# A third buffer for a mixture's float32 weight loads, and gathers and scatters queued behind the last subtraction on GpSimd

## The chip, the cores and the metric

The kernel runs on one core of a Trainium2 chip. The metric is the device time of one execution in microseconds (us). The runs of the kernel before took 1203.83, 1204.78 and 1204.12 us, median 1204.12.

Names of the engines in the profile: PE is TensorE's matmuls and PEld its weight loads, DVE is VectorE, ACT is ScalarE, POOL is GpSimd, SP is SyncE, which here only issues DMAs.

## What is computed

The reference, cut to what matters. The input x has shape (4, 2496, 256), which is 9984 tokens of 256.

```python
x = np.fft.fft(np.fft.fft(x, axis=1), axis=2).real            # over the sequence, then over the 256

# first mixture: 8 experts, each takes 1248 tokens
order = np.argsort(-(x @ w_gate).flatten())                   # greedy, best (token, expert) pairs first
...                                                           # a token once, an expert 1248 times
for e in range(8):
    out[mask[e]] = np.maximum(x[mask[e]] @ w1[e], 0) @ w2[e]  # 256 -> 1024 -> 256

# second mixture, on the first's output
e_idx = np.argmax(x @ w_gate2, axis=1)
for e in range(8):
    out[e_idx == e] = gate_w * sigmoid(x @ w_output_gate)[:, e] * (np.maximum(x @ w1[e], 0) @ w2[e])
```

## The kernel before

Up to about 250 us the kernel computes the transform and the scores of the first mixture's gate. Then a selection finds, expert by expert, which 1248 tokens an expert takes; it runs on VectorE with some matmuls (L525 to L542, the places of the tokens at L669 to L671). From 760 to 1164 us the second mixture runs. Between the two lies the stretch that the change touches: the first mixture's eight experts, one after the other, and beside them the preparation of the second.

Matrices are kept as two float16 halves, a high one and a low one (the rest), and each product takes three matmuls. So each tile that is copied costs a pass for the high half and one for the low half.

For each expert k of the first mixture (class Moe1):

- `prepare` loads its six float32 weight tiles (wf, `Weights.part`, L756, issued by SP; which expert is a number that the chip works out, so an ISA instruction reads it first), waits in the plan for the selection, and gathers the tokens by index in ten indirect DMAs that POOL issues (xg, L873). The tokens go to the layers in three chunks of 384, 384 and 480. Transposes (L890) and their copies by ACT and DVE (L892, L893) make xt of each chunk.
- `weights` cuts the wf tiles into halves (wh; a part of it on POOL, L788).
- `hidden` runs the first layer in eight units per chunk (matmuls L824 into ph, three PSUM buffers). ACT makes the high half (ht, L904). The low half is made by DVE (L910), or, in the odd units for which `fk // 2 < HP[k]`, by POOL: ACT copies once more into hf (L907, three buffers) and POOL subtracts (L908). HP is 3, 3, 3, 4, 2, 0, 0, 0 for experts 0 to 7.
- `out_block` runs the second layer (matmuls L832 into py, two PSUM buffers), and ACT copies each result to yr (L921).
- `route` picks the second mixture's expert for each token, writes the results to DRAM (yd, SP, L970 and L971), works out each token's place in the second mixture's lists (L979), and puts entries of eight bytes there in ten indirect DMAs that POOL issues (lst, L985).

Beside it `keep2` (L1083 to L1109) prepares the second mixture's weights: 8 experts of 4 parts, 32 parts of 512 KB in float32. SP loads a part into one of two buffers (`g_0`, `g_1`, L756), ACT makes its high half (wp, L1102), DVE the low half (L1103), and SP stores both halves to DRAM (wsd, L1104). The load of part n + 2 is issued behind the store of part n, so that it finds the buffer free.

```python
nc.scalar.activation(h[:, q, 0], fs[q], AF.Copy, scale=64.0)
nc.vector.scalar_tensor_tensor(h[:, q, 1], fs[q], 64.0, h[:, q, 0], op0=OP.mult, op1=OP.subtract)
nc.sync.dma_start(self.wsd[e, :, q], h[:, q])
if e < 7 or q < 2:
    load(e + q // 2, (q + 2) % 4)
```

What sets the order of the work: the program is traced with a planner's clock. The matmul units of the first mixture advance the clock (`flow.unit`), and the side jobs above are generators that yield how long they want to wait on it. So the numbers yielded (GY, SY, KY and the like) set between which units a step is queued; nothing on the chip waits for them. A scheduler then orders each engine's instructions. `issue_after(i)` in it places an instruction behind i in the queue; that too is an order, not a wait. The loads of `keep2` are placed behind the latest of the first mixture's weight loads (`self.W.at`).

Of the kernel before, what the change touches and what calls it, by code (L numbers as in the profile page):

```python
# [10 lines left out]
F32 = mybir.dt.float32  # L11
# [715 lines left out]
GG = 8.0  # L727
RY = 5.0
GY = 2.0
SY = 2.5  # L730
XY = 2.0
KY = 7.0
# [103 lines left out]
class Moe1:  # L836
    CH = ((0, 3), (3, 3), (6, 4))

    def __init__(self, tc, nc, a, xd, yd, lst, wsd, sel, pools, consts, bufs):
        self.tc, self.nc, self.a, self.xd, self.yd, self.lst, self.sel = tc, nc, a, xd, yd, lst, sel  # L840
        self.P = pools
        self.c = consts
        p = pools["keep"]
        self.base = p.tile([128, 8], F32, name="m_base")
        nc.vector.tensor_copy(self.base, consts["eoff"])
        self.wg = p.tile([128, 2, 2, 16], F16, name="m_wg")
        self.scat = []
        self.W = Weights(nc, pools["wts"], pools["stage"], a["moe_w1"], a["moe_w2"], a["moe_w2t"])
        self.wsd, self.bufs = wsd, bufs
        self.W2 = Weights(nc, pools["wts"], pools["stage"], a["moe2_w1"], a["moe2_w2"])  # L850
# [10 lines left out]
    def load(self, k):  # L861
        e = self.nc.sync.value_load(self.sel.ei[0:1, k:k + 1], min_val=0, max_val=7)
        return self.W.load(e)

    def gather(self, k):
        nc = self.nc
        idx = self.sel.idx[k]
        xg = self.P["xg"].tile([128, 10, D], F32, name="xg")

        def steps():  # L870
            for t in range(10):
                m = 128 if t < 9 else 96
                nc.gpsimd.indirect_dma_start(out=xg[:m, t], out_offset=None, in_=self.xd,  # L873
                                             in_offset=bass.IndirectOffsetOnAxis(ap=idx[:m, t:t + 1], axis=0))
                yield
        return xg, steps()

# [20 lines left out]
    def hidden(self, xt, n, wh, k):  # L898
        nc = self.nc
        ht = self.P["ht"].tile([128, 2, 8, 512], F16, name="ht")  # L900
        for fk in range(8):
            ph = self.P["psum"].tile([128, 512], F32, name="ph", bufs=3)
            ffn1_unit(nc, xt, wh[0], fk, n, ph[:, :n])
            self.act = nc.scalar.activation(ht[:, 0, fk, :n], ph[:, :n], AF.Relu)  # L904
            if fk % 2 and fk // 2 < HP[k]:
                hf = self.P["work"].tile([128, 480], F32, name="hf", bufs=HFB)
                nc.scalar.activation(hf[:, :n], ph[:, :n], AF.Relu)  # L907
                nc.gpsimd.tensor_sub(ht[:, 1, fk, :n], hf[:, :n], ht[:, 0, fk, :n])  # L908
            else:
                nc.vector.scalar_tensor_tensor(ht[:, 1, fk, :n], ph[:, :n], 0.0, ht[:, 0, fk, :n],  # L910
                                               op0=OP.max, op1=OP.subtract)
            yield n * 6 / 2400.0
        self.ht = ht
# [10 lines left out]
    def route(self, yr, k):  # L924
# [54 lines left out]
        nc.vector.tensor_copy(pi, px)  # L979
        nc.vector.tensor_add(self.base, self.base, pr[:, 80:88])  # L980
        self.counted = k
        ent = self.lst.rearrange("r (s w) -> (r s) w", w=2)
        for t in range(10):
            m = 128 if t < 9 else 96
            s = nc.gpsimd.indirect_dma_start(out=ent, in_=en[:m, t], in_offset=None,  # L985
                                             out_offset=bass.IndirectOffsetOnAxis(ap=pi[:m, t:t + 1], axis=0))
            for o in self.scat:
                self.tc.declare_no_dep(s.ins, o.ins, reason="every row has a place of its own")
            self.scat.append(s)
            yield 2.0 if k == 6 else 8.0 if k == 7 else 4.0  # L990

    def ffn(self, k, flow):

        wh = self.ws.pop(k)
        xg, xt = self.xgs.pop(k)
        yr = self.P["yr"].tile([128, 10, YW], F32, name="yr")
        self.nc.gpsimd.memset(yr[96:128, 9], 0.0)
        hts, nxt = {}, []

        def unit(d):  # L1000
            flow.unit(d)
            while nxt and nxt[0][0] <= 0:
                if next(nxt[0][1], 1):
                    nxt.pop(0)
                    self.cut += 1
                break
            if nxt:
                nxt[0][0] -= 1

        for c in range(4):  # L1010
            if c < 3:
                cur = xt
                if c < 2:
                    xt, st = self.xt(xg, c + 1)
                    nxt.append([3, st])
                for d in self.hidden(cur[0], cur[1], wh, k):
                    unit(d)
                hts[c] = self.ht
            else:
                self.tail = k  # L1020
            if c > 0:
                flow.until(lambda: self.gated >= k)
                t0, nt = self.CH[c - 1]
                for t in range(nt):
                    m = min(128, CAP - (t0 + t) * 128)
                    for d in self.out_block(hts[c - 1], t0 + t, t * 128, m, wh, yr):
                        unit(d)

        def rest():
            yield from self.route(yr, k)  # L1030
            self.routed = k
        flow.add(rest(), 1.0, prio=PR)
# [8 lines left out]
    def prepare(self):  # L1041

        for k in range(8):
# [4 lines left out]
                self.sel.placed = k  # L1048
            yield lambda: self.sel.placed >= k
            xg, steps = self.gather(k)  # L1050
            for t, _ in enumerate(steps):
                yield 0.0 if t < 4 else GY
            yield lambda: self.tail >= k - 1
            xt, steps = self.xt(xg, 0)
            for _ in steps:
# [1 line left out]
            self.xgs[k] = (xg, xt)  # L1057
            yield lambda: k in self.ws
            self.ready = k

    def weights(self):

# [19 lines left out]
    def keep2(self):  # L1082

        nc = self.nc
        yield lambda: self.at >= KEEP[0]
        h = self.P["wts"].tile([128, 4, 2, 1024], F16, name="wp", bufs=1)
        fs = [self.bufs[q % 2].rearrange("p a b -> p (a b)")[:, :1024] for q in range(4)]

        def load(e, q):
            with self.tc.issue_after(self.W.at.ins):  # L1090
                self.W2.part(fs[q], slice(e, e + 1), q)

        load(0, 0)
        load(0, 1)
        for e in range(8):
            if e and KEEP[e] > self.at:
                yield lambda: self.at >= KEEP[e]
            else:
                yield KY
            for q in range(4):  # L1100
                with self.tc.issue_after(self.act.ins):
                    nc.scalar.activation(h[:, q, 0], fs[q], AF.Copy, scale=64.0)  # L1102
                nc.vector.scalar_tensor_tensor(h[:, q, 1], fs[q], 64.0, h[:, q, 0], op0=OP.mult, op1=OP.subtract)  # L1103
                nc.sync.dma_start(self.wsd[e, :, q], h[:, q])  # L1104
                if e < 7 or q < 2:
                    load(e + q // 2, (q + 2) % 4)
                if q < 3:
                    yield KY
            self.kept = e  # L1109

    def run(self, flow, m2):
        self.cut = 0
        self.gated = -1
        self.counted = self.kept = -1
# [430 lines left out]
```

## Time and profile before

| | |
|---|---|
| median of the runs | 1204.12 us |
| the profiled execution | 1203.47 us, of which the span is 1201.7 us |
| PE busy | 1119.0 us (93%), 9823 matmuls |
| PEld busy | 821.8 us (68%) |
| DVE busy | 729.9 us (61%) |
| POOL busy | 498.4 us (41%) |
| ACT busy | 440.8 us (37%) |
| moved by DMA | 212.96 MB, mean 177 GB/s |

The span runs from the first to the last instruction that the profiler shows; 1.8 us of the execution lie around it. Busy times are those of each engine over the span; engines overlap. All times in the text count from the span's start. The granted clock is a share of TensorE's full clock, 1.00 being 2.4 GHz and 0.50 being 1.2 GHz.

### The profile page before, as it was taken

To read this page: it belongs to the slowest core of one execution; us is meant where nothing else is said; L and a number is where in the kernel's file an instruction comes from. 1 tells how busy PE (TensorE), PEld (TensorE's weight loads), DVE (VectorE), ACT (ScalarE), POOL (GpSimd) and SP (SyncE) were. 2 spreads that over 40 slices of the span, in tenths; PEclk is the share of its full clock that TensorE was granted. 3 is DMA by queue.
4 is the path that set the end of the run, shared out by engine and by line. 5 is a ranking of instruction groups with operands and counts; after the bars stand their busy time and mean duration, and the time that the engine had idled before them with its cause. 6 is when DMAs were issued, how large, how long until landed. Compare 5 with 4: busy or idle time off the path is not lost.

```text
span 1201.7 us, 24544 instructions
## 1 busy us (share of the span) xinstructions
PE 1119.0 (93%) x9823; PEld 821.8 (68%) x9823; DVE 729.9 (61%) x1786; ACT 440.8 (37%) x936; POOL 498.4 (41%) x471
## 2 busy tenths in 40 slices
PE   7998879979898989899798999999999999999998
PEld 4653546756667657567485767766766799999997
DVE  5866779897978977867456574434334343434343
ACT  3423334263452734345354443222223122222221
POOL 3825351468373781433306045643332334343331
PEclk8999989999999999989899999999999999999999
DMA  7834722243341571686838458444343366788782
GB/s 257 334 122 157 264 80 88 61 128 65 106 90 64 155 182 56 150 271 155 239 129 244 162 134 295 139 157 153 119 172 114 119 250 234 273 311 331 308 332 92
DMA packets 80036, 212.96 MB, mean 177 GB/s; under 512 B 11850, under 2 KB 48986, under 8 KB 69168
## 3 DMA queue, kind: packets, MB, share of 16 engines
q1 hardware_dynamic: 65360, 180.46, 44.5%
q0 software_dynamic: 14560, 30.91, 8.5%
q8 instruction: 78, 1.28, 0.5%
q14 instruction: 38, 0.31, 0.1%
HBM read 162.22 MB, written 50.42 MB: 177 GB/s over the span
## 4 chain that ended last, share of the span: by engine, by line
PE 28%; issue 23%; DVE 16%; POOL 10%; DMA 9%; ACT 2%; POOLq 0%; SPq 0%; DVEq 0%; ACTq 0%
PE py L832 14%; PE ph L824 9%; DMA g<-moe_w 6%; DMA out<-ot,tbrow 3%; POOL xg L1336 3%; POOL out L1381 2%; POOL g L1336 2%; DVE s_msk L525 2%; DVE ht L910 2%; PE px L693 1%; POOL xg L873 1%; DVE wp L1103 1%; PE pt L890 1%; POOL lst L985 1%; PE sp L531 1%
## 5 line engine op out<-in xcount | busy, mean ns | idle before, releaser
L832 PEld LDWEIGHTS <-ht 128*128 128x128 f16 (+1 forms) x3912 | 380.6, 99 | 61.3 <-issue 6.0
L824 PE MATMUL ph<-xt,wh 128*128 128x384 f16 (+4 forms) x2352 | 386.1, 316 | 26.9 <-DVE ht L910 14.8
L832 PE MATMUL py<-wh,ht 128*128 128x272 f16 (+2 forms) x3264 | 393.8, 277 | 4.2 <-ACT yr L921 4.2
L824 PEld LDWEIGHTS <-wh 128*128 128x128 f16 x2352 | 211.2, 99 | 148.8 <-issue 38.8
L1368 ACT ACTIVATE ht<-ph 128x512 f16<-128x512 f32 x166 | 99.1, 597 | 315.8 <-PE ph L824 315.8
L1369 DVE SCALAR_TENSOR_TENSOR ht<-ph,ht 128x512 f16<-128x512 f32 x166 | 114.8, 691 | 126.7 <-ACT ht L1368 126.7
L985 POOL DMA_INDIRECT lst<-r_en,r_pi x80 | 87.5, 1094 | 145.5 <-DVE r_pi L979 89.5
L904 ACT ACTIVATE ht<-ph 128x384 f16<-128x384 f32 (+1 forms) x192 | 98.4, 516 | 85.0 <-PE ph L824 76.9
L1381 POOL DMA_INDIRECT out<-ot,tarow x54 | 54.5, 1010 | 158.8 <-DVE ot L1380 152.1
L873 POOL DMA_INDIRECT xg<-xd,s_idx x80 | 87.9, 1099 | 34.9 <-issue 20.8
L910 DVE SCALAR_TENSOR_TENSOR ht<-ph,ht 128x384 f16<-128x384 f32 (+1 forms) x147 | 85.0, 585 | 19.4 <-ACT ht L904 19.1
L908 POOL TENSOR_TENSOR ht<-hf,ht 128x384 f16<-128x384 f32 (+1 forms) x45 | 48.7, 1090 | 93.2 <-ACT hf L907 80.0
L305 PE MATMUL big<-y,tab 128*128 128x36 f16 (+3 forms) x660 | 79.4, 273 | 1.1 <-DVE y L256 1.1
L921 ACT ACTIVATE yr<-py 128x272 f32<-128x272 f32 x80 | 31.3, 394 | 121.0 <-PE py L832 103.6
L832 PE MATMUL py<-wp,ht 128*128 128x256 f16 x648 | 73.7, 273 | 0.0
L824 PE MATMUL ph<-xt,wp 128*128 128x256 f16 (+2 forms) x624 | 72.9, 277 | 0.0
L1381 POOL DMA_INDIRECT out<-ot,tbrow x29 | 28.9, 997 | 101.9 <-DVE ot L1380 96.1
L1380 DVE TENSOR_SCALAR ot<-py,g 128x256 f32<-128x256 f32 x45 | 21.7, 483 | 70.6 <-PE py L832 70.6
L824 PEld LDWEIGHTS <-wp 128*128 128x128 f16 x624 | 51.4, 98 | 19.1
L1103 DVE SCALAR_TENSOR_TENSOR wp<-g,wp 128x1024 f16<-128x1024 f32 x32 | 39.9, 1247 | 32.2 <-ACT wp L1102 32.1
L305 PEld LDWEIGHTS <-tab 128*128 128x128 f16 x660 | 38.8, 97 | 30.0 <-issue 3.0
L525 DVE SCALAR_TENSOR_TENSOR s_msk<-s_vv,lo,s_jw 128x1280 f16<-128x1280 f32 x35 | 57.5, 1643 | 0.8
(254 smaller groups left out, 1313.2 us busy)
## 6 DMA issues: line engine op xcount, KB each, us to landing
wh<-wsd SPq DMA_DIRECT2D x50, 1024.0 KB, 6.0
wp<-wsd SPq DMA_DIRECT2D x26, 1024.0 KB, 6.0
wf<-moe_w SPq DMA_DIRECT2D x32, 512.0 KB, 6.0
g<-moe_w SPq DMA_DIRECT2D x32, 512.0 KB
wsd<-wp SPq DMA_DIRECT2D x32, 512.0 KB, 5.1
xa<-xa SPq DMA_DIRECT2D x8, 1280.0 KB, 11.1
xd<-xr SPq DMA_DIRECT2D x20, 512.0 KB, 4.8
yd<-yr SPq DMA_DIRECT2D x8, 1156.5 KB
```

What stands on the lines that cost most here:

```text
L305: self.nc.tensor.matmul(dst, self.tabs[par][k][:, cs, c, u], self.y[par][:, cs, w, c, bs, qs], start=(n == 0), stop=(n == 3 * NCH - 1))
L525: nc.vector.scalar_tensor_tensor(m, self.vv[:, :, None].to_broadcast(sh), lo, self.jw[:, r, None, :].to_broadcast(sh), op0=OP.subtract, op ...
L824: Flow.pe = nc.tensor.matmul(dst, w1[:, dk, a, fk * 128:fk * 128 + 128], xt[:, b, dk, :n], start=(k == 0), stop=(k == 5))
L832: Flow.pe = nc.tensor.matmul(dst, ht[:, a, fk, t0:t0 + m], w2[:, fk // 4, b, fk % 4], start=(fk == 0 and a == 0 and b == 0), stop=(fk == 7 ...
L873: nc.gpsimd.indirect_dma_start(out=xg[:m, t], out_offset=None, in_=self.xd, in_offset=bass.IndirectOffsetOnAxis(ap=idx[:m, t:t + 1], axis=0))
L904: self.act = nc.scalar.activation(ht[:, 0, fk, :n], ph[:, :n], AF.Relu)
L910: nc.vector.scalar_tensor_tensor(ht[:, 1, fk, :n], ph[:, :n], 0.0, ht[:, 0, fk, :n], op0=OP.max, op1=OP.subtract)
L985: s = nc.gpsimd.indirect_dma_start(out=ent, in_=en[:m, t], in_offset=None, out_offset=bass.IndirectOffsetOnAxis(ap=pi[:m, t:t + 1], axis=0))
L1336: nc.gpsimd.indirect_dma_start(out=g[:, h], out_offset=None, in_=self.yd, in_offset=bass.IndirectOffsetOnAxis(ap=row[:, 0, u + h:u + h + 1 ...
L1368: nc.scalar.activation(hi, src, AF.Relu)
L1369: nc.vector.scalar_tensor_tensor(lo, src, 0.0, hi, op0=OP.max, op1=OP.subtract)
L1381: st = nc.gpsimd.indirect_dma_start(out=self.out, in_=ot, in_offset=None, out_offset=bass.IndirectOffsetOnAxis(ap=row[:, 1, u + h:u + h + ...
```

## The change

There are three parts to it.

1. A third buffer for the float32 parts of the second mixture (tile `k_2`). Part n uses buffer n mod 3. The load of part n + 3 is issued after the conversion of part n, ahead of that part's store; before, part n + 2 was issued behind it. The load is still placed behind the latest weight load of the first mixture.
2. Each gather and each scatter is placed behind the last subtraction (L908) traced so far on POOL (`behind`).
3. The planner's steps for gathers and scatters. For experts 1 to 7 three gathers are placed first, and the other seven are a side job of their own, 3 us of the planner's clock apart (2 for expert 1). The transposes of the second and third chunk are traced only when all ten gathers are. The scatters of experts 0 to 5 begin 7 us later in the plan, and stand 3.5 rather than 4 apart.

```diff
@@ steps of the plan
+GL = 3.0
+SD = 7.0
@@ class Moe1
+    def behind(self):
+        return self.tc.issue_after(self.sub.ins) if self.sub else ExitStack()
@@ gather (each of ten)
-                nc.gpsimd.indirect_dma_start(out=xg[:m, t], out_offset=None, in_=self.xd,
+                with self.behind():
+                    nc.gpsimd.indirect_dma_start(out=xg[:m, t], out_offset=None, in_=self.xd,
@@ hidden
-                nc.gpsimd.tensor_sub(ht[:, 1, fk, :n], hf[:, :n], ht[:, 0, fk, :n])
+                self.sub = nc.gpsimd.tensor_sub(ht[:, 1, fk, :n], hf[:, :n], ht[:, 0, fk, :n])
@@ route (ten scatters)
+        if k < 6:
+            yield SD
-            s = nc.gpsimd.indirect_dma_start(out=ent, in_=en[:m, t], in_offset=None,
+            with self.behind():
+                s = nc.gpsimd.indirect_dma_start(out=ent, in_=en[:m, t], in_offset=None,
...
-            yield 2.0 if k == 6 else 8.0 if k == 7 else 4.0
+            yield 2.0 if k == 6 else 8.0 if k == 7 else 3.5
@@ ffn
                 if c < 2:
+                    flow.until(lambda: self.got[k] == 10)
                     xt, st = self.xt(xg, c + 1)
@@ prepare
-            for t, _ in enumerate(steps):
-                yield 0.0 if t < 4 else GY
+            self.got[k] = 0
+            if k:
+                for _ in range(3):
+                    next(steps)
+                    yield GY
+                self.flow.add(self.others(k, steps), GL)
+            else:
+                for t, _ in enumerate(steps):
+                    yield 0.0 if t < 4 else GY
+                self.got[k] = 10
...
+    def others(self, k, steps):
+        for t in range(3, 10):
+            next(steps)
+            self.got[k] = t + 1
+            yield GL if k > 1 else GY
@@ keep2
-        fs = [self.bufs[q % 2].rearrange("p a b -> p (a b)")[:, :1024] for q in range(4)]
+        fs = [t.rearrange("p a b -> p (a b)")[:, :1024] for t in self.bufs]
+        fs.append(self.P["keep"].tile([128, 1024], F32, name="k_2", bufs=1))
-        def load(e, q):
+        def load(n):
             with self.tc.issue_after(self.W.at.ins):
-                self.W2.part(fs[q], slice(e, e + 1), q)
+                self.W2.part(fs[n % 3], slice(n // 4, n // 4 + 1), n % 4)
-        load(0, 0)
-        load(0, 1)
+        for n in range(3):
+            load(n)
...
+                n = 4 * e + q
+                f = fs[n % 3]
...
+                if n < 29:
+                    load(n + 3)
                 nc.sync.dma_start(self.wsd[e, :, q], h[:, q])
-                if e < 7 or q < 2:
-                    load(e + q // 2, (q + 2) % 4)
```

How the order of the instructions moves is shown at three places. In the names a part's buffer is g_2072 (buffer 0), g_2073 (1) and k_5714 (the new one); a part's shape is 128x1024 or 128x4x256.

SP's queue at the turn from expert 3 to expert 4, before: the first mixture's last weight loads (wf), the store of the results (yd), and the loads of parts 13 (g_2073) and 14 (g_2072).

```order
L1104 DMA wsd<-wp 128x2048
L756 ISA
L756 DMA wf<-moe_w2t 128x1024
L970 DMA yd<-yr 128x9x257
L756 ISA
L756 DMA wf<-moe_w2t 128x1024
L756 DMA g_2073<-moe_w 128x1024
L756 DMA g_2072<-moe_w 128x4x256
L971 DMA yd<-yr 96x257
```

The same place now, with the loads of parts 14 (k_5714), 15 (g_2072) and 16 (g_2073).

```order
L1135 DMA wsd<-wp 128x2048
L758 ISA
L758 DMA wf<-moe_w2t 128x1024
L758 ISA
L758 DMA wf<-moe_w2t 128x1024
L758 DMA k_5714<-moe_w 128x4x256
L758 DMA g_2072<-moe_w 128x4x256
L977 DMA yd<-yr 128x9x257
L978 DMA yd<-yr 96x257
L758 DMA g_2073<-moe_w 128x1024
```

Part 13's load has gone ahead of the expert's last weight loads, parts 14 and 15 stand where 13 and 14 stood, and the store of the results stands behind them.

ACT's queue at the same turn, before: the conversions L1102 are of parts 13, 14, 15 and 16, and L921 copies results of the second layer (yr).

```order
L904 ACTIVATE ht<-ph 128x384 x2
L799 ACTIVATE wt<-wf 128x256
L1102 ACTIVATE wp<-g_2073 128x1024
L921 ACTIVATE yr<-py 128x272
L1102 ACTIVATE wp<-g_2072 128x1024
L921 ACTIVATE yr<-py 128x272 x2
L904 ACTIVATE ht<-ph 128x480
L1102 ACTIVATE wp<-g_2073 128x1024
L904 ACTIVATE ht<-ph 128x480 x4
L1102 ACTIVATE wp<-g_2072 128x1024
```

The same place now, where the conversions (L1131) are of parts 14, 15 and 16.

```order
L801 ACTIVATE wt<-wf 128x256
L911 ACTIVATE ht<-ph 128x384
L899 ACTIVATE xt<-pt 128x480
L911 ACTIVATE ht<-ph 128x384 x2
L1131 ACTIVATE wp<-k_5714 128x1024
L1131 ACTIVATE wp<-g_2072 128x1024
L928 ACTIVATE yr<-py 128x272 x3
L911 ACTIVATE ht<-ph 128x480 x5
L1131 ACTIVATE wp<-g_2073 128x1024
```

Part 13's conversion has moved some ten instructions ahead and stands above these rows; those of 14 and 15 stand together ahead of three copies of results, and 16 behind five units of the third chunk.

POOL's queue where it gathers the tokens of expert 4 (index tile s_idx_90) while expert 3 computes, before: gathers are L873, scatters L985, subtractions L908.

```order
L788 TENSOR_TENSOR wh<-wf,wh 128x2x256
L985 DMA lst<-r_en,r_pi 81920x2
L908 TENSOR_TENSOR ht<-hf,ht 128x384
L985 DMA lst<-r_en,r_pi 81920x2 x2
L873 DMA xg<-xd,s_idx_90 128x256 x8
L908 TENSOR_TENSOR ht<-hf,ht 128x384
L873 DMA xg<-xd,s_idx_90 128x256
L908 TENSOR_TENSOR ht<-hf,ht 128x384
L873 DMA xg<-xd,s_idx_90 96x256
L985 DMA lst<-r_en,r_pi 81920x2
L997 MEMSET yr 32x272
```

The same place now (gathers L880, scatters L995, subtractions L915).

```order
L880 DMA xg<-xd,s_idx_90 128x256 x3
L915 TENSOR_TENSOR ht<-hf,ht 128x384
L995 DMA lst<-r_en,r_pi 81920x2
L1007 MEMSET yr 32x272
L915 TENSOR_TENSOR ht<-hf,ht 128x384
L880 DMA xg<-xd,s_idx_90 128x256
L995 DMA lst<-r_en,r_pi 81920x2
L880 DMA xg<-xd,s_idx_90 128x256 x2
L995 DMA lst<-r_en,r_pi 81920x2
L880 DMA xg<-xd,s_idx_90 128x256
L995 DMA lst<-r_en,r_pi 81920x2
L915 TENSOR_TENSOR ht<-hf,ht 128x480
```

Eight gathers stood in a row ahead of a subtraction; three do now, and the others have moved behind the subtractions and alternate with the scatters.

## Rows read from the trace of the kernel before

**Rows 1.** Stage table, last stage and whole span: stretch, us, busy us, PEclk, DMA share, GB/s.

```profile
760.00:1164.10 404.10, 403.62 (x3514) 322.67 (x3512) 159.33 (x265) 105.82 (x187) 147.62 (x145) 1.00 0.58 216
...
sum 1201.70, PE 1118.98 PEld 821.79 DVE 729.94 ACT 440.80 POOL 498.42; mean PE 124.33 PEld 91.31 DVE 81.10 ACT 48.98 POOL 55.38
```

**Rows 2.** Waits of PE, 490 to 660: us in total, times, longest.

```profile
PE ph L824 <- DVE ht L910: 10.0, 3, 6.6
PE ph L824 <- ACT hf L907: 5.4, 1, 5.4
PE py L832 <- ACT yr L921: 4.2, 3, 2.5
```

**Rows 3.** Waits of ACT, whole span.

```profile
ACT wp L1102 <- DMA g<-moe_w: 40.2, 17, 8.3
...
ACT hf L907 <- POOL ht L908: 7.7, 2, 5.3
```

**Rows 4.** Timeline of PE: start, us, engine, line, operation, [idle before <- releaser].

```profile
373.82 0.19 PE L542 MATMUL sp<-r,ch 128*128 128x8 f16 x1 [3.07 <-DVE r L538]
...
440.70 0.56 PE L824 MATMUL ph<-xt,wh 128*128 128x480 f16 x2 [3.79 <-ACT hf L907]
...
457.10 0.49 PE L890 MATMUL pt<-cf,xg 128*128 128x128 f32 x3
...
512.82 2.56 PE L824 MATMUL ph<-xt,wh 128*128 128x480 f16 x6 [5.43 <-ACT hf L907]
...
570.30 2.94 PE L832 MATMUL py<-wh,ht 128*128 128x272 f16 x24 [1.57 <-ACT yr L921]
...
586.45 4.96 PE L824 MATMUL ph<-xt,wh 128*128 128x480 f16 x12 [6.58 <-DVE ht L910]
...
655.50 1.38 PE L824 MATMUL ph<-xt,wh 128*128 128x480 f16 x6 [1.82 <-DVE ht L910]
```

**Rows 5.** Timeline of ACT, conversions of parts 6, 7, 13 and 14.

```profile
506.54 1.06 ACT L1102 ACTIVATE wp<-g 128x1024 f16<-128x1024 f32 x1 [4.99 <-DMA g<-moe_w]
...
510.79 1.06 ACT L1102 ACTIVATE wp<-g 128x1024 f16<-128x1024 f32 x1 [2.45 <-DMA g<-moe_w]
...
568.90 1.06 ACT L1102 ACTIVATE wp<-g 128x1024 f16<-128x1024 f32 x1 [0.92 <-DMA g<-moe_w]
...
573.11 1.06 ACT L1102 ACTIVATE wp<-g 128x1024 f16<-128x1024 f32 x1 [2.86 <-DMA g<-moe_w]
```

**Rows 6.** Timeline of SP, loads of part 6, and of parts 13 and 14.

```profile
494.10 1.24 SPq L756 DMA_DIRECT2D g<-moe_w  x1
...
558.66 2.35 SPq L756 DMA_DIRECT2D g<-moe_w  x2
```

**Rows 7.** Windows of 4 us: stretch, us, busy us, PEclk, DMA share, GB/s.

```profile
440.00:444.00 4.00, 3.30 (x20) 1.59 (x20) 2.57 (x6) 3.92 (x9) 3.67 (x4) 0.72 0.17 58
...
512.00:516.00 4.00, 3.18 (x9) 1.32 (x9) 3.85 (x11) 1.81 (x5) 3.08 (x4) 0.50 0.89 263
516.00:520.00 4.00, 4.00 (x30) 1.97 (x28) 1.85 (x3) 2.90 (x7) 3.09 (x4) 0.89 1.02 400
...
560.00:564.00 4.00, 4.00 (x30) 2.81 (x29) 3.96 (x9) 2.51 (x5) 3.29 (x3) 1.00 1.15 216
...
584.00:588.00 4.00, 1.55 (x4) 0.56 (x4) 2.92 (x4) 1.95 (x4) 1.30 (x3) 0.50 0.89 323
588.00:592.00 4.00, 4.00 (x23) 1.76 (x22) 1.88 (x2) 2.07 (x5) 0.00 (x0) 0.50 0.44 151
```

**Rows 8.** Timeline of POOL, two of the gathers for expert 4.

```profile
438.16 0.95 POOL L873 DMA_INDIRECT xg<-xd,s_idx  x1 [0.30 <-issue]
...
442.27 1.85 POOL L873 DMA_INDIRECT xg<-xd,s_idx  x1 [0.16 <-ACT wp L1102]
```

**Rows 9.** Timeline of DVE, the shift at L670 twice.

```profile
369.36 1.02 DVE L670 TENSOR_SCALAR pi<-pi 128x80 int32<-128x80 int32 x1
...
514.38 0.20 DVE L670 TENSOR_SCALAR pi<-pi 128x80 int32<-128x80 int32 x1
```

More of the change, by code (lines that the diff above doesn't have):

```diff
@@ L846, in __init__ @@
         self.wg = p.tile([128, 2, 2, 16], F16, name="m_wg")
-        self.scat = []
+        self.scat, self.sub = [], None
         self.W = Weights(nc, pools["wts"], pools["stage"], a["moe_w1"], a["moe_w2"], a["moe_w2t"])
@@ L872, in steps @@
                 m = 128 if t < 9 else 96
-                nc.gpsimd.indirect_dma_start(out=xg[:m, t], out_offset=None, in_=self.xd,
-                                             in_offset=bass.IndirectOffsetOnAxis(ap=idx[:m, t:t + 1], axis=0))
+                with self.behind():
+                    nc.gpsimd.indirect_dma_start(out=xg[:m, t], out_offset=None, in_=self.xd,
+                                                 in_offset=bass.IndirectOffsetOnAxis(ap=idx[:m, t:t + 1], axis=0))
                 yield
@@ L984, in route @@
             m = 128 if t < 9 else 96
-            s = nc.gpsimd.indirect_dma_start(out=ent, in_=en[:m, t], in_offset=None,
-                                             out_offset=bass.IndirectOffsetOnAxis(ap=pi[:m, t:t + 1], axis=0))
+            with self.behind():
+                s = nc.gpsimd.indirect_dma_start(out=ent, in_=en[:m, t], in_offset=None,
+                                                 out_offset=bass.IndirectOffsetOnAxis(ap=pi[:m, t:t + 1], axis=0))
             for o in self.scat:
@@ L1100, in keep2 @@
             for q in range(4):
+                n = 4 * e + q
+                f = fs[n % 3]
                 with self.tc.issue_after(self.act.ins):
-                    nc.scalar.activation(h[:, q, 0], fs[q], AF.Copy, scale=64.0)
-                nc.vector.scalar_tensor_tensor(h[:, q, 1], fs[q], 64.0, h[:, q, 0], op0=OP.mult, op1=OP.subtract)
+                    nc.scalar.activation(h[:, q, 0], f, AF.Copy, scale=64.0)
+                nc.vector.scalar_tensor_tensor(h[:, q, 1], f, 64.0, h[:, q, 0], op0=OP.mult, op1=OP.subtract)
+                if n < 29:
+                    load(n + 3)
                 nc.sync.dma_start(self.wsd[e, :, q], h[:, q])
-                if e < 7 or q < 2:
-                    load(e + q // 2, (q + 2) % 4)
                 if q < 3:
@@ L1111, in run @@
     def run(self, flow, m2):
+        self.got, self.flow = {}, flow
         self.cut = 0
```

## The prediction

> **What bounds the kernel now.** I read the stage table first. TensorE (PE) is busy 1118.98 of 1201.70 us, so 82.7 us are all that better ordering can give back; the stage from 760 to 1164 has 0.5 us of them [rows 1]. So I read next who stops PE between 490 and 660, the stretch in which ScalarE (ACT) converts most of the second mixture's 32 float32 weight parts: 10.0, 5.4 and 4.2 us, 19.6 in all [rows 2]. All three releasers are ACT, or VectorE behind ACT: PE stands because ACT's queue stands. In the table of waits ACT stands for the parts' loads (g<-moe_w) for 40.2 us in 17 waits, the longest 8.3 [rows 3]. The second line there is another cause: ACT waits 7.7 us for a buffer that GpSimd's (POOL's) subtraction at L908 must free.
>
> The stalls themselves stand in PE's timeline: 3.07 us before 373.82, 3.79 before 440.70, 5.43 before 512.82, 6.58 before 586.45 and 1.82 before 655.50 [rows 4]. On ACT, part 6 is converted at 506.54 and part 7 at 510.79, each after a wait for its load; parts 13 and 14 at 568.90 and 573.11 likewise [rows 5]. SP issued part 6 at 494.10, and parts 13 and 14 together at 558.66 [rows 6]; before that they stood in SP's queue behind the first mixture's last weight load.
>
> A stall costs a second time. In 512 to 516 the granted clock is 0.50, which is 1.2 of 2.4 GHz, after PE had stood 5.4 us; a busy microsecond there does half the work. The loss, busy time times the missing share, is 3.18 x 0.5 + 4.00 x 0.11 = 2.0 us after the stall at 512; (1.55 + 4.00) x 0.5 = 2.8 us after the one at 586; 3.30 x 0.28 = 0.9 us after the one at 440 [rows 7].
>
> **The change, part by part.** *Third buffer.* No conversion, load or store is added; each load moves one conversion earlier on SP. A load can only start when the conversion three before it has freed its buffer, and SP stands for that with the store behind it; that store is next needed in the second mixture, so I cost this wait at nothing. What it buys depends on which load is late.
> - Stall at 512: part 6 is now issued before SP reaches the first mixture's last weight load, and part 7 takes part 6's place at 494.10. Part 6 landed 12.4 us after that [rows 5, 6]. If part 7 does the same, ACT leaves its conversion at 507.6 instead of 511.85, 4.3 us earlier, and 1.2 us of the stall stay; if the fewer scatters in that stretch help, none. I take 1.0: gain 5.4 - 1.0 = 4.4, and 2.0 of clock. Bounds: 3.2 without the clock, 7.4.
> - Stalls from 568 to 587: part 13 is loaded and converted ahead; parts 14 and 15 are issued ahead of the big result store and take, at worst, the places of 13 and 14, which landed at 568.90 and 573.11 [rows 5]. The order on ACT now has both conversions ahead of three result copies (yr) that PE waits for. So the 6.6 us go, and with them the smaller wait for L910 just before (10.0 - 6.6 - 1.8 = 1.6 [rows 2, 4]); the wait for yr, 4.2 - 2.5 - 0.2 = 1.5 [rows 2], may stay, or grow until part 15 is converted: PE stood from 570.30 - 1.57 = 568.73 on [rows 4], so 573.11 + 1.06 - 568.73 = 5.4. I take 2.0 left of 9.7, nearer to the present 1.5 than to 5.4, as the store of the results no longer stands in front. Gain 7.7, clock 2.8 less 0.5: 10.0. Bounds 9.7 - 5.4 = 4.3, and 9.7 + 2.8 = 12.5.
> - Stalls at 642 and 655: part 22 takes the place of 21 and waits as that did, so the 2.5 us for yr stay; part 23 is early and the 1.8 us go. Bounds 0 and 4.3.
> - Moved conversions: parts 13 and 21 now stand between the first layer's units, where a conversion costs ACT 1.06 us [rows 5] with PE and VectorE both full. I take 1.0 for both; bounds 0 and 2 x 1.06.
>
> How fast a load lands decides half of this. In 560 to 564 the DMA engines are busy throughout (1.15) and move 216 GB/s; in 516 to 520, as busy (1.02), 400 [rows 7]. The first stretch has the list's scatters of eight bytes in it. The Trainium skill ("DMA: Bandwidth & Descriptors", Specifications) gives a core about 358 GB/s of HBM and warns that transfers under 512 B do not run at line rate. By its 358 in place of 216, part 7's 12.4 us would be an estimated 7.5, the 3.0 us left above would vanish, and the sum would be 3.5 us better. The trace shows both less and more than 358, so I stay with the measured places.
>
> *Gathers and scatters behind the last subtraction.* Before 440.70 PE waits for ACT's copy hf, ACT for a free hf buffer, and that for a subtraction queued behind eight gathers, each 0.95 us and 0.30 idle [rows 8], 10 us in all. Now at most three gathers stand between two subtractions of that chunk. The 3.79 us go but for 0.3: 3.5 and 0.9 of clock, 4.4. Bounds 0 and 4.7. The last gather before was issued at 442.27 [rows 8] and comes later now, behind subtractions of the second chunk; its rows belong to the third chunk, while even the first chunk's transposes begin only at 457.10 [rows 4]. The work between is the cover; without it PE would stand for each late gather as it stood for the late loads.
>
> Subtractions also run earlier, and that moves a second cost. The cast and shifts at L669 to L671 take 1.02 us each while POOL subtracts, 0.20 when it does not [rows 9]; three such put VectorE late by 2.5 us before PE's 3.07 us wait at 373.82. Those three subtractions now run earlier, beside other VectorE work. Gain 0 to 3.1; elsewhere new meetings of the same kind can cost as much. I take 2.0 for the whole of it, bounds -6 and 4.
>
> Sum: 6.4 + 10.0 + 1.8 - 1.0 + 4.4 + 2.0 = 23.6 us. The profiled execution took 1203.5 us (span 1201.7), 0.6 under the median of 1204.1; from the median the forecast is 1180.5 us. After 760 PE has no idle time to lose, so I pass the gain on to the end undiminished.
>
> **Rivals.** *The engines, not the order, set the landing.* If the DMA engines are the limit, a load issued earlier lands when the queue drains, whatever its place. For it: 1.15 busy at 560. Against it: 400 GB/s at 516. Then the stall at 512 stays whole, of the 9.7 us at 568 to 587 only 4.3 are gained, without clock, and the sum is 0 + 4.3 + 1.8 - 1.0 + 4.4 + 2.0 = 11.5: 1193 us.
>
> *Subtractions meet VectorE.* By the code 27 subtractions stand in experts 2 to 4 (three chunks with 3, 4 and 2 each); each that meets a VectorE operation on SBUF can hold it for 1.02 - 0.20 = 0.8 us more [rows 9]. If half of them newly do so in the selection's chain, 14 x 0.8 = 11 us go back: 1192 us. The Trainium skill ("SBUF — State Buffer", on the shared port pair) says the pair that VectorE and GpSimd share is an exclusive lock, held for the whole instruction, so that the loser blocks fully. By that rule each meeting costs a full subtraction rather than a share; the rows at 369 agree. Against it: the number of subtractions is unchanged, and they meet VectorE already.
>
> *ACT stands in front of yr (slower).* The new order puts two or three conversions in a row ahead of PE's result copies at four places (parts 9 and 10; 14 and 15; 17 to 19; 24 to 26). With PE's two result buffers a late load there stops PE at once. If each place waited as long as ACT's longest wait now, 8.3 us [rows 3], and lost 2.8 of clock, the cost would be 44 us and the time 1225; it decides from 6 us at each place. Against it: the last of each row has its load issued a conversion earlier than now.
>
> *It does nothing.* If the loads still stood behind the first mixture's, times would stay. The order shows parts 6, 13 and 21 ahead of it; 3 in 100.
>
> **How the numbers follow.** Forecast 0.70; engines set the landing 0.13; subtractions meet VectorE 0.09; ACT in front of yr 0.05; nothing 0.03. A measurement of this kernel can tell about 0.2%, 2.4 us, from no change. Faster by more: 0.91 (part of the small cases allows for my bounds, so 0.90). Same 0.04, slower 0.06. The range reaches from 1172 (all the upper bounds give 7.4 + 12.5 + 4.3 + 4.7 + 4 = 32.9, which is 1171) to 1193 (the two rivals that halve the gain); what is left out is some 0.15.
>
> **What would show it.** Right: ACT's waits for the loads fall from 40 us to under 15; no stall over 3 us between 490 and 660; the clock at 512 and 584 near 1.0; PE's wait for hf at 440 gone; one wait of about 2.5 us for yr near 620 to 640 left. Wrong: ACT's conversions of parts 7, 14 or 15 still end waits of over 4 us; PE's waits for yr above 8 us in all; transposes at L890 (now L897) waiting for gathers; more than 20 us new VectorE time in operations that meet subtractions.

## The result, and the profile after

The changed kernel took 1193.15 us (median of 6 runs, 1188.98 to 1194.08), the kernel before 1203.97 in the same comparison: a ratio of 0.9909, 95% interval 0.9887 to 0.9930. That is 10.8 us faster, where 23.6 were forecast. The first four of the experiments ran on a chip on which the kernel before took 1262 us, so all experiments are compared by their ratios to the kernel before on the same chip.

One correction to the text on the change: what it calls the turn from expert 3 to expert 4 is, by the code's numbers from 0, the one from 4 to 5. The rows there are the right ones.

The forecast was 1180.5 us, with a range from 1172 to 1193; the measured time lies just beyond its upper end. The stage table after, for [rows 1]. PE's idle time in the span has fallen from 82.7 to 1191.10 - 1116.70 = 74.4 us; the stage from 760 on had and has next to none, so the gain lies ahead of it.

```profile
760.00:1153.50 393.50, 393.18 (x3454) 317.06 (x3453) 154.99 (x258) 102.82 (x182) 140.38 (x138) 1.00 0.58 215
...
sum 1191.10, PE 1116.70 PEld 820.08 DVE 729.38 ACT 440.47 POOL 510.00; mean PE 124.08 PEld 91.12 DVE 81.04 ACT 48.94 POOL 56.67
```

The waits of PE from 490 to 660, which were 10.0, 5.4 and 4.2 [rows 2], have changed their releaser and not their sum: 19.6 before, 18.6 now.

```profile
PE py L834 <- ACT yr L928: 13.7, 2, 10.0
PE ph L826 <- ACT hf L914: 4.9, 1, 4.9
```

ACT's waits for the parts, which were 40.2 us [rows 3], have fallen to 16.6 + 4.0. The third line, which puts the wait of part 16's conversion down to a store, has the wrong releaser (below).

```profile
ACT wp L1131 <- DMA g<-moe_w: 16.6, 4, 5.7
...
ACT wp L1131 <- DMA k<-moe_w: 4.0, 2, 2.3
...
ACT wp L1131 <- DMA wsd<-wp: 2.9, 1, 2.9
```

In PE's timeline after, the stalls of [rows 4] at 371 and 437 are gone. Shorter waits of PE for VectorE's selection have come in their place: from 350 to 490 all its waits together were 13.0 us before and are 9.5 now. The other stalls stand:

```profile
502.69 1.76 PE L826 MATMUL ph<-xt,wh 128*128 128x480 f16 x4 [4.91 <-ACT hf L914]
...
587.01 3.33 PE L834 MATMUL py<-wh,ht 128*128 128x272 f16 x14 [10.04 <-ACT yr L928]
...
634.81 2.51 PE L834 MATMUL py<-wh,ht 128*128 128x272 f16 x13 [3.65 <-ACT yr L928]
```

ACT's timeline shows what PE waited for. The first row is part 7 [rows 5], the next four are parts 16 to 19. PE's next two results are copied (yr, L928) only behind the last of them.

```profile
499.91 1.06 ACT L1131 ACTIVATE wp<-g 128x1024 f16<-128x1024 f32 x1 [5.70 <-DMA g<-moe_w]
...
570.68 1.06 ACT L1131 ACTIVATE wp<-g 128x1024 f16<-128x1024 f32 x1 [2.89 <-DMA wsd<-wp]
...
575.58 1.06 ACT L1131 ACTIVATE wp<-k 128x1024 f16<-128x1024 f32 x1 [1.76 <-DMA k<-moe_w]
579.77 1.06 ACT L1131 ACTIVATE wp<-g 128x1024 f16<-128x1024 f32 x1 [3.14 <-DMA g<-moe_w]
585.62 1.06 ACT L1131 ACTIVATE wp<-g 128x1024 f16<-128x1024 f32 x1 [4.79 <-DMA g<-moe_w]
586.58 0.67 ACT L928 ACTIVATE yr<-py 128x272 f32<-128x272 f32 x2
```

The second row says that part 16 waited for a store. The trace's own semaphore updates say otherwise (each DMA raises its semaphore sixteen times as it lands). By the code the store that it needs is that of part 12, four parts before it, in the same quarter of wp; this was issued at 535.76, and its last update came at 538.94. The store that the view names, part 13's, was issued at 553.85, and its last update came at 571.77, after the conversion had begun at 570.68. The last update of part 16's own load, issued at 552.51, came at 570.66. So it waited for its load, as 17, 18 and 19 did: their loads' last updates came at 575.49, 579.67 and 585.51, and the stores that they need had landed before. With 2.9 us more, ACT's waits for loads come to 23.5. In the profile of the same kernel run again (after_again) the view itself names the load for part 16:

```profile
568.88 1.06 ACT L1131 ACTIVATE wp<-g 128x1024 f16<-128x1024 f32 x1 [1.76 <-DMA g<-moe_w]
```

SP's timeline gives the issue of these loads: part 7 behind the store of results and a weight load, then parts 17, 18 and 19. From issue to conversion it is 13.5 us for part 7, then 18.7, 21.1 and 12.6. Part 19 is issued only at 573.02, because its load needs the buffer of part 16, which is converted at 570.68.

```profile
484.79 0.38 SPq L977 DMA_DIRECT2D yd<-yr  x1
486.02 0.33 SPq L758 DMA_DIRECT2D wf<-moe_w2t  x1
486.39 1.25 SPq L758 DMA_DIRECT2D g<-moe_w  x1
...
556.90 0.33 SPq L758 DMA_DIRECT2D k<-moe_w  x1
...
558.70 0.38 SPq L758 DMA_DIRECT2D g<-moe_w  x1
...
573.02 0.39 SPq L758 DMA_DIRECT2D g<-moe_w  x1
```

The windows of 4 us after, for [rows 7]: the clock falls to 0.50 of 2.4 GHz behind the stall as it did before, and costs 0.99 x 0.50 + 4.00 x 0.39 = 2.1 us in the last two rows, where it was 2.8. Between 556 and 568 the DMA engines are busy throughout and move 113 to 192 GB/s; from 576 on, as busy, 387.

```profile
556.00:560.00 4.00, 4.00 (x37) 3.39 (x35) 4.00 (x6) 1.26 (x3) 3.09 (x4) 1.00 1.15 113
560.00:564.00 4.00, 4.00 (x26) 2.27 (x24) 2.70 (x6) 1.40 (x3) 2.65 (x3) 1.00 1.08 192
...
576.00:580.00 4.00, 0.97 (x18) 0.81 (x17) 1.29 (x1) 0.86 (x2) 1.64 (x3) 1.00 1.03 387
...
584.00:588.00 4.00, 0.99 (x5) 0.68 (x5) 1.29 (x3) 2.33 (x6) 0.00 (x0) 0.50 0.87 340
588.00:592.00 4.00, 4.00 (x24) 2.74 (x22) 0.70 (x3) 0.03 (x1) 0.00 (x0) 0.61 0.47 190
```

Two profiled executions can't be subtracted whole. The first 50 us are the same code in both kernels, and the clock there was 0.86 before and 1.00 after (stage tables of before, then of after). The matmuls at 184 us, where the change has done nothing yet, already stand 3.1 us earlier. The other profiled executions start at 0.86, 0.93 or 1.00, whichever kernel it is, so stalls are compared here one by one, and times by the medians.

```profile
0.00:50.00 50.00, 41.03 (x362) 26.86 (x362) 31.84 (x47) 19.95 (x38) 31.01 (x21) 0.86 0.75 270
```

```profile
0.00:50.00 50.00, 41.44 (x392) 26.52 (x393) 32.78 (x50) 20.04 (x39) 31.23 (x21) 1.00 0.81 295
```

### The profile page after: what moved, and what is told of

Its sections match the earlier page's. It is cut to its first block, busy times and chain, and to the rows that moved or that the text cites. A ratio compares the mean times of both kernels' runs of the same rounds, so it can differ in the third digit from the quotient of the medians.

```text
span 1191.1 us, 24549 instructions
## 1 busy us (share of the span) xinstructions
PE 1116.7 (94%) x9823; PEld 820.1 (69%) x9823; DVE 729.4 (61%) x1786; ACT 440.5 (37%) x936; POOL 510.0 (43%) x471
## 4 chain that ended last, share of the span: by engine, by line
PE 35%; issue 20%; DVE 17%; DMA 8%; POOL 7%; ACT 2%; POOLq 0%; SPq 0%; DVEq 0%; ACTq 0%
PE py L834 17%; PE ph L826 13%; DMA g<-moe_w 3%; DMA out<-ot,tbrow 3%; DVE s_msk L525 2%; POOL out L1411 2%; POOL xg L1366 2%; DVE ht L917 2%; POOL g L1366 2%; DMA wsd<-wp 2%; PE px L693 1%; PE pt L897 1%; DVE hb L686 1%; DVE wp L1132 1%; DVE wt L802 1%
## 5 line engine op out<-in xcount | busy, mean ns | idle before, releaser
L834 PE MATMUL py<-wh,ht 128*128 128x272 f16 (+2 forms) x3264 | 395.4, 278 | 13.7 <-ACT yr L928 13.7
L995 POOL DMA_INDIRECT lst<-r_en,r_pi x80 | 91.6, 1145 | 135.9 <-DVE r_pi L986 78.0
L880 POOL DMA_INDIRECT xg<-xd,s_idx x80 | 90.9, 1137 | 40.1 <-issue 18.8
L915 POOL TENSOR_TENSOR ht<-hf,ht 128x384 f16<-128x384 f32 (+1 forms) x45 | 52.0, 1158 | 91.1 <-ACT hf L914 77.8
L928 ACT ACTIVATE yr<-py 128x272 f32<-128x272 f32 x80 | 31.4, 395 | 137.0 <-PE py L834 120.7
L1410 DVE TENSOR_SCALAR ot<-py,xg 128x256 f32<-128x256 f32 x38 | 18.4, 483 | 58.5 <-PE py L834 58.5
```

The lines of the kernel that those rows point to most:

```text
L834: Flow.pe = nc.tensor.matmul(dst, ht[:, a, fk, t0:t0 + m], w2[:, fk // 4, b, fk % 4], start=(fk == 0 and a == 0 and b == 0), stop=(fk == 7 ...
L915: self.sub = nc.gpsimd.tensor_sub(ht[:, 1, fk, :n], hf[:, :n], ht[:, 0, fk, :n])
```

## The experiments

The standing theory after the result: the queueing gave what was forecast, and the third buffer's gain was lost again on ACT, where its conversions stand in a row ahead of the copies that PE waits for (theories P and F). The rival: the DMA engines are full between 550 and 590, so that no order of loads or conversions matters there (theory E).

### The two halves alone

The queueing with the planner's steps, two buffers; run twice. And the third buffer alone; run twice.

```diff
 # queue_alone, queue_alone_2: the changed kernel with keep2 as before
-            for n in range(3):
-                load(n)
+            load(0, 0)
+            load(0, 1)
...
 # buf_alone, buf_alone_2: the kernel before with the changed keep2
+        fs.append(self.P["keep"].tile([128, 1024], F32, name="k_2", bufs=1))
```

Queueing: 

> The queueing and the planner's steps of the change, with two buffers as before. Theory A (the queueing carries the gain, the third buffer is worth nothing): 1193 to 1197 us, the wait for hf near 437 and the wait at 371 gone, the stalls near 507 and 568 to 587 as in the kernel before. Theory B (each part carries about half): 1197 to 1200. Theory C (the buffer carries it): 1201 to 1205.

> The queueing and the planner's steps with two buffers once more. Theory G: 1194 to 1198 us where the kernel before takes 1204, so that the change as it stands owes the queueing nearly all its gain. Rival (the buffer as it stands carries half of it): 1198 to 1201.

Buffer: 

> The third buffer alone, gathers and scatters as before. Theory A: 1201 to 1205 us; the stall near 507 still 4 to 6 us, and 8 to 11 us between 568 and 587, whichever part is late. Theory B: 1197 to 1200. Theory C: 1190 to 1194, with the stalls near 437 and 371 still there.

> The third buffer alone once more, beside the other of this call. Theory P (its conversions in a row give its gain back): 1198 to 1203 us where the kernel before takes 1204; the stall near 507 down to 1 to 2 us as with the copies counted, and one of 8 us or more for yr after 580, which is not in the kernel before. Theory E (no load lands earlier): the stalls of the kernel before at 507 and 568 to 587 as they were, 1202 to 1206.

Measured: the queueing 0.9942 (0.9906 to 0.9978) and 0.9957 (0.9934 to 0.9980), the second 1198.91 us; the buffer 0.9981 (0.9948 to 1.0014) and 0.9957 (0.9936 to 0.9977), the second 1199.94. So the queueing comes out at 5.2 to 7.0 us of 1204, and the buffer at 2.3 to 5.2, of which the lower figure is not clear of nothing. Together that is some 10 us, the gain of the change. Theory B fits best: the queueing is not worth all of it (A), and the buffer does not carry it (C), but is worth far less than the 17.2 us that were forecast for it (6.4 + 10.0 + 1.8 - 1.0). The buffer's second profile shows how (PE's timeline): the stall near 507 is smaller, 3.88 where it was 5.43, though not the 1 to 2 that were expected, and one of 9.84 has come, for yr.

```profile
508.93 2.25 PE L824 MATMUL ph<-xt,wh 128*128 128x480 f16 x6 [3.88 <-ACT hf L907]
...
593.23 3.10 PE L832 MATMUL py<-wh,ht 128*128 128x272 f16 x13 [9.84 <-ACT yr L921]
```

### The conversions between the copies

One attribute more: a conversion is placed behind the last of ACT's copies traced, yr included, and not behind the last ht alone. The order of PE's work in the trace stays the same from the first matmul to the last. Beside it the changed kernel itself, the same with two buffers, and the same with each store ahead of its load.

```diff
 # conv_yr
-        nc.scalar.activation(yr[:m, t], py[:m, :YW], AF.Copy, scale=1.0 / 256.0)
+        self.act = nc.scalar.activation(yr[:m, t], py[:m, :YW], AF.Copy, scale=1.0 / 256.0)
 # conv_yr_two: and keep2 with two buffers as before
 # conv_yr_store: conv_yr, and
+                nc.sync.dma_start(self.wsd[e, :, q], h[:, q])
                 if n < 29:
                     load(n + 3)
-                nc.sync.dma_start(self.wsd[e, :, q], h[:, q])
```

> The changed kernel once more, beside the kernels of this call. All theories: a ratio of 0.988 to 0.994 to the kernel before, PE stalls of about 5 us in the third chunk of expert 2's or 3's first layer (hf) and of 8 to 12 us for yr after the turn to expert 4.

> The changed kernel with the copies of results (yr) counted among the ACT instructions behind which a conversion is placed, so that conversions of parts 17 to 19 and 24 to 26 stand one by one between the copies and not in a row ahead of them. Theory P (their place on ACT made the 10.0 us stall): that stall falls under 3 us and the 3.6 us one goes too, 8 to 14 us faster than the changed kernel, a ratio of 0.978 to 0.985 to the kernel before. Theory E (the DMA engines are full, so the loads are late whatever stands behind them): the stall is cut in smaller ones at the next copies with 8 us or more in sum, 0.987 to 0.994.

> The copies counted and the queueing as in the change, but two buffers as before. It tells what the third buffer is worth once conversions don't stand in a row. Theory F (the buffer is worth the forecast's 10 us or more, and its bunched conversions gave that back): 6 us or more slower than with three buffers. Theory E: within 3 us of it.

> The same, and each store ahead of its load. Theory D (the store that stood behind a waiting load held up part 16): 2 to 5 us faster than the kernel with only the copies counted. Theory P: the store's wait is off PE's path once the conversions stand apart, no difference over 2 us.

Measured, with 1204.47 us for the kernel before: the changed kernel again 1191.99, 0.9895 (0.9861 to 0.9928); with the copies counted 1175.31, 0.9750 (0.9720 to 0.9780); that with two buffers 1194.05, 0.9905 (0.9876 to 0.9934); that with the stores first 1174.43, 0.9744 (0.9715 to 0.9772).

So 16.7 us come from where the conversions stand, more than theory P expected, and E falls. The third buffer, compared between the two kernels with the copies counted, is worth 1194.05 - 1175.31 = 18.7 us: theory F. In ACT's timeline with the copies counted, the conversions of parts 17 and 18 stand between the copies:

```profile
574.11 0.40 ACT L928 ACTIVATE yr<-py 128x272 f32<-128x272 f32 x1 [0.42 <-PE py L834]
575.00 1.06 ACT L1131 ACTIVATE wp<-k 128x1024 f16<-128x1024 f32 x1 [0.48 <-DMA k<-moe_w]
576.89 0.40 ACT L928 ACTIVATE yr<-py 128x272 f32<-128x272 f32 x1 [0.84 <-PE py L834]
...
583.08 0.40 ACT L928 ACTIVATE yr<-py 128x272 f32<-128x272 f32 x1 [0.90 <-PE py L834]
583.37 1.05 ACT L1131 ACTIVATE wp<-g 128x1024 f16<-128x1024 f32 x1
```

Part 17 is no earlier than in the changed kernel: issued at 557.07, it ends ACT's wait at 575.00, after 17.9 us where it was 18.7. PE does not stand for it, because the copy that it needs is not behind it. From 490 to 650, one wait of PE is left:

```profile
PE ph L826 <- ACT hf L914: 4.9, 1, 4.9
```

Putting the stores first changes nothing that can be told: 0.9 us between two kernels whose intervals overlap, as theory P had it. D started from the wait for a store that the view showed, and no conversion there waited for one. Putting the stores first in the changed kernel, without the copies counted, had shown no more:

> The changed kernel, but each store ahead of the load that goes with it. In the changed kernel part 16's conversion ends a 2.9 us wait for a store (wsd<-wp) that stands behind a load which waits for its buffer. Theory D (that order of SP's queue makes parts 16 to 19 late): the wait for the store goes, PE's 10.0 us stall near 577 falls to 6 or less, 1187 to 1191 us. Theory E (the DMA engines are full there, so the order of SP's queue does not matter): the stall stays within 1.5 us of 10, 1191 to 1195.

Measured: 0.9906 (0.9867 to 0.9945), the changed kernel's own ratio. The interval is too wide to rule out D's smaller end there. Its profile does show what D named: PE's longest wait for yr in that place is 2.8 us. But it was taken on the chip of the 1262 us, where PE also stands 5.2 us between 490 and 660 for nothing that the profile shows, and it has no counterpart of the changed kernel on that chip. With the copies counted, nothing of it is left to see.

### One place alone

The copies counted for parts 16 to 19 only.

```diff
 # conv_e4
-                with self.tc.issue_after(self.act.ins):
+                with self.tc.issue_after((self.copy if e == 4 else self.act).ins):
```

> The changed kernel with the copies of results counted for the conversions of parts 16 to 19 alone. Theory P1 (the row of 17 to 19 ahead of the copies is the one place that costs): the stall of 8 to 10 us for yr near 577 goes, the one of 3.7 us near 631 stays, 1179 to 1183 us where the kernel before takes 1204. Theory P2 (each place counts alike, 24 to 26 as much): 1184 to 1188. Theory E: 1189 to 1193.

Measured: 1180.16 us, 0.9799 (0.9765 to 0.9833). P1 holds: against the changed kernel's 0.9895 and 0.9909, this one row costs 0.0096 to 0.0110 of 1204, 11.6 to 13.2 us, give or take some 5 by the intervals. What is left to the 0.9750, some 6 us, belongs to all the other conversions that conv_yr moves, which were not tried one by one. The waits of PE from 490 to 650 in this kernel:

```profile
PE ph L826 <- ACT hf L914: 3.7, 1, 3.7
PE py L834 <- ACT yr L928: 2.4, 1, 2.4
```

### The buffer without the queueing, and part 7

```diff
 # buf_conv_yr: the kernel before, the changed keep2, and conv_yr's line
 # anchor4: conv_yr_store, and in Weights.load
-            self.at = self.part(f, bass.ds(e, 1), q)
+            ld = self.part(f, bass.ds(e, 1), q)
+            if q < 4:
+                self.at = ld
```

> The third buffer with the copies counted, but gathers and scatters as before. Theory G (the queueing is worth 7 to 10 us by itself, whatever the buffers do): 1181 to 1186 us where the kernel before takes 1204, with the stalls near 371 and 437 back. Theory H (those stalls are made up for later): within 3 us of the kernel with both, 1173 to 1178.

> The copies counted, each store ahead of its load, and a part's load placed behind the fourth of an expert's six weight loads and not behind the sixth, so that part 7 is issued ahead of the store of the results and the last two weight loads. Theory J (the wait of 2.7 to 4.9 us for hf near 497 is a load that stands behind others on SP): the wait falls under 1 us, 1170 to 1172.5 us. Theory E (the engines are full, the weight loads are then late in its place): 1173.5 to 1177, with a wait of 2 us or more for wh or the gate's weights.

Measured, with 1205.24 us for the kernel before: the buffer with the copies counted and no queueing 1181.08, 0.9809 (0.9780 to 0.9838); part 7 ahead 1170.15, 0.9720 (0.9691 to 0.9749). In this pair G holds: the queueing is worth 0.0059, 7 us. Alone with two buffers (queue_alone_2) it missed G's 1194 to 1198 and fell into its rival's range. J holds by its wait and its range; the 0.0024 that this kernel gains on conv_yr_store is not clear of noise by itself. In the first kernel the stall near 507 has come down to 1.59, near the 1.2 us that the prediction worked out:

```profile
508.19 1.38 PE L824 MATMUL ph<-xt,wh 128*128 128x480 f16 x6 [1.59 <-ACT hf L907]
```

With the queueing, PE is there earlier (502.69 - 4.91 = 497.78 in the changed kernel, 512.82 - 5.43 = 507.39 before [rows 4], so 9.6 us). The place on SP that part 7's load takes is earlier only by 494.10 - 486.39 = 7.7 us, because it stands behind the store of results and a weight load. In SP's timeline of the last kernel it is issued ahead of both, and no wait of PE is left between 490 and 650.

```profile
467.22 0.43 SPq L758 DMA_DIRECT2D g<-moe_w  x1
471.81 0.35 SPq L758 DMA_DIRECT2D wf<-moe_w2t  x1
484.91 0.37 SPq L979 DMA_DIRECT2D yd<-yr  x1
```

This kernel is the fastest of all: 2.8% faster than the one before, and about 1.8% than the changed one.

### Behind the subtraction, and nothing else

```diff
 # behind_only, behind_only_2: the kernel before, and for gathers and scatters
+                with self.behind():
...
 # without GL, SD, the three gathers first and the spacing of 3.5
```

> The kernel before with each gather and scatter queued behind the last subtraction, and nothing of the planner's steps or the buffer. Theory A1 (the place behind the subtraction is what matters): the 3.8 us wait near 437 goes, 1197 to 1200 us. Theory A2 (the thinning of the gathers, three and then one at a time, is what matters): 1201 to 1204, the wait at 437 still 2 us or more, because a row of gathers behind one subtraction still stands ahead of the next.

> The kernel before with gathers and scatters behind the last subtraction and nothing else, once more. Theory A1 (the place behind the subtraction is what matters): the waits near 371 and 437 are gone and it is within 3 us of the queueing with the planner's steps. Theory A2 (the thinning matters): 1201 to 1204, a wait for hf of 2 us or more left near 437.

Measured: 0.9958 (0.9917 to 0.9999) on the one chip, 1.0022 (0.9999 to 1.0045) on the other; they disagree, and whether it is worth a little or nothing stays open. The second profile shows why it need not gain: the wait for hf near 437 is gone, as A1 had it, but PE then stands 7.83 us for hf near 507, where it stood 5.43, and VectorE is late at other places. At L611 an operation on one element a partition takes 159 ns as a rule, and once 2810 (the line's own view, min, median and max; then DVE's timeline):

```profile
L611 DVE SCALAR_TENSOR_TENSOR ab<-s_wr,ab x8: 148/159/2810, 112.9 to 489.4; 128x1 f32<-128x1 f32 x8
...
410.81 2.81 DVE L611 SCALAR_TENSOR_TENSOR ab<-s_wr,ab 128x1 f32<-128x1 f32 x1
```

In POOL's timeline three of its operations stand back to back over just that time, 410.81 to 413.62:

```profile
410.71 0.91 POOL L913 TENSOR_TENSOR ht<-hf,ht 128x384 f16<-128x384 f32 x1
411.58 1.15 POOL L788 TENSOR_TENSOR wh<-wf,wh 128x512 f16<-128x512 f32 x1
412.69 0.90 POOL L913 TENSOR_TENSOR ht<-hf,ht 128x384 f16<-128x384 f32 x1
```

A stall of PE of 2.8 us follows. With the planner's steps the same queueing gave 5 to 7 us. Which of the steps does it was not tried alone.

## Why the prediction was partly wrong

- **The step that failed** is the one on the stalls from 568 to 587. It followed parts 14 and 15, found both conversions ahead of three copies, and closed with "So the 6.6 us go". For these two it was right: they ran at 554 and 555, and PE did not wait. But parts 16 to 19 come next. The changed order put 17 to 19 in a row ahead of the copies, and the loads of 16 to 18 were issued into or just ahead of the slow stretch from 556 to 568, that of 19 only when 16 was converted. 9.7 us of stalls were replaced by one of 10.04, with 2.1 us of clock behind it, instead of the 2.0 that were to be left. Of the 10.0 us forecast for this place hardly any came; conv_e4 gives back 11.6 to 13.2.
- **That was the rival "ACT stands in front of yr"**, which had a chance of 0.05 and was priced at four places. Its price was right for one place: 8.3 + 2.8 = 11.1 us, measured 11.6 to 13.2 (with part 16's conversion moved too). Of its four places only this one cost so much, so it lowered the gain and did not turn the sign. What was held against it, that the last load of a row is issued a conversion earlier, did not help: 12.6 to 21.1 us from issue to conversion. A rival whose places can fail one by one should have been priced one by one, and the forecast's chance given to the cases between.
- **The stall at 512** is the second term that was mis-sized: 4.4 + 2.0 forecast, 5.43 - 4.91 = 0.5 measured in stall. The sum took the buffer's gain together with that of the queueing, as if the load's time were fixed by the clock on the wall and PE's too. Both move, and PE by 1.9 us more; the load took 13.5 us instead of 12.4. For the buffer without the queueing the 1.2 us that it worked out depend on how long the load takes: 1.59 are left in buf_conv_yr, where part 7 takes 505.42 - 493.99 = 11.4 us, and 3.88 in buf_alone_2, where it takes 506.16 - 492.44 = 13.7. The measured gain lies below the lower bound of 3.2, for which no working is given.
- **642 and 655**: 2.5 us for yr were to stay, and 3.65 stand at 634.81, behind part 22 as forecast. The 1.8 at 655 are gone.
- **"That store is next needed in the second mixture, so I cost this wait at nothing"** was wrong in its reason: by the code the store also frees a quarter of wp for the conversion four parts later. The cost of nothing stood all the same: no conversion of parts 16 to 19 waited for such a store.
- **The queueing** was right: 4.4 + 2.0 forecast, 5.2 to 7.0 us measured alone, and both stalls that it was to remove are gone.
- **"The engines, not the order, set the landing"** came out at the measured time, 1193, but that is chance. Its sum gains 4.3 of the 9.7 us at 568 to 587, and none of them was gained in stall. The order does set when a part is there: part 14, issued at 548.10, was converted at 554, 5.9 us after its issue by its load's last update, where part 13 took 568.90 - 558.66 = 10.2 [rows 5, 6]. And where loads are late all the same, conv_yr shows that PE need not wait for them.
- **The signs** told it: ACT's waits for loads stayed above 15 us, three stalls over 3 us stood between 490 and 660, part 7's conversion ended a wait of 5.70, and PE's waits for yr came to 13.7 us, above 8.
- The Trainium skill ("DMA: Bandwidth & Descriptors", Specifications) gave, by its 358 GB/s, an estimated 7.5 us for part 7. The trace does not agree: 13.5.

## What to carry to other kernels

A buffer that is loaded further ahead also lets a scheduler queue its consumer further ahead. Look where the consumers now stand on their in-order engine, follow every one of them through the stretch and not only those that were late before, and tie each behind an instruction that the critical engine needs first. In conv_yr a load that came 17.9 us after its issue cost PE nothing, because nothing that PE needed stood behind the instruction that waited for it. And check the releaser that a view names against the other loads and stores in flight: here it named a store, where a load had landed.

## What the runs showed of the hardware

- Between 556 and 568 the DMA engines were 1.07 to 1.15 busy and moved 113 to 192 GB/s, and from 576 on 387 at 1.03. The ten scatters of eight-byte entries for expert 4 are issued from 547 to 561, but GpSimd's queue (q0) has only 2.6% of the engines' time from 556 to 568; SP's (q1) has the rest. By the trace's table of DMA packets, 117 of the 16 x 12 = 192 us are packets of 1028 bytes, the rows of the store of results: 143 ns each, where they took 51 from 484 to 488 with nothing beside them. SP's packets of 4096 bytes took 325 ns there, and 170 from 576 to 584. From 488 to 492, with no packet of q0, the rate is 211 GB/s as well. From 564 to 568, with the store nearly done and 4.1% for q0, it is still 190. So the store of results and the scatters are both candidates, and neither was tried alone.

```profile
488.00:492.00 4.00, 4.00 (x35) 2.70 (x33) 4.00 (x17) 2.33 (x6) 3.22 (x3) 1.00 1.09 211
```

```profile
q1 hardware_dynamic: 1142, 1.95, 107.1%
q0 software_dynamic: 218, 0.02, 2.6%
```

- One VectorE operation of 0.16 us lasted 2.81 us, through three GpSimd operations back to back. The prediction had priced such a meeting at 0.8. The Trainium skill ("SBUF — State Buffer", "SBUF: two separate sides") says that the shared port pair is locked for a whole instruction. The trace agrees, and in this one case the operation kept out did not get in between two of the other's.
- The granted clock of the first 50 us differs between executions of the same code (0.86 and 1.00). In the two profiles compared, what follows at 184 us stands 3.1 us apart.
